# Moving weight sums and up items, and starting the sorted pairs five points sooner, in a routing attention and Strassen feed-forward kernel

## The chip, the core and the metric

The kernel runs on one core of one Trainium2 chip. The metric is the device time of one execution in microseconds (us). The engines of the core work in parallel, each on its own queue in order: TensorE (PE in the profile, its weight loads PEld), VectorE (DVE), ScalarE (ACT), GpSimd (POOL) and SyncE (SP), which here only issues DMAs. An instruction waits on semaphores for what it needs, and whatever stands behind it on its engine waits with it.

## What is computed

Attention with 4 batches, 8 heads, 768 tokens and 64 dimensions, in which a query sees only the keys of its own cluster (16 clusters per head, each token's cluster being the centroid with the largest product), and then a feed-forward layer with a hard swish:

```python
mask = q_assign[:, :, :, None] == k_assign[:, :, None, :]
scores = np.where(mask, 0.125 * q @ k.T, -1e9)      # per batch and head
attn = softmax(scores) @ v
x = attn.transpose(0, 2, 1, 3).reshape(3072, 512)
h = x @ w_in                                        # 512 -> 2048
g = h * np.clip(h + 3.0, 0.0, 6.0) / 6.0
out = g @ w_out                                     # 2048 -> 512
```

The weights come as 64-bit floats and are decoded on the chip.

## The kernel before

**Pairs.** Two heads make a pair: 16 pairs, four for each batch. Pairs 0 to 7 (batches 0 and 1) are done with full scores and a mask in a main loop; pairs 8 to 15 are sorted by cluster, so that a tile of 128 queries meets only three tiles of keys (a band).

**The main loop** (in `fast_path`) counts n in steps of two, 12 numbers for a pair. A step issues the scores, exponentials and key sums of two tiles (the key sums are adds on POOL, L430 and L433), the products with the values two tiles back, at two places per pair the division by the row sums (`sum_up`: products into a scratch bank, then reciprocal L473 and product L474 on VectorE), and the preparation of the next pair (`prep_items`: three turns of queries and keys into columns, L320, copied out by ScalarE, L326; cluster scores, L337; one hots, L348 to L357 and L379). The scratch of these, the `ph` of the up items and later X share the two banks of `psum_m`, in turn. Each step also issues a share of the weight decoding (five steps for each of 32 chunks: L232, L238, L248, L254 and L259 on VectorE, L228 and L244 on ScalarE), and at its end the eight half sums of w_out (`weight_sums`, L523).

**Feed-forward.** Tokens go through in 12 blocks of 256 (three per batch). A block is a list of 30 half items: 8 up items and 7 down items, each with a begin and an end. In the first block (u < 8) an up item is a plain product into `ph` (L597), a lift on ScalarE (L499) and a clip on VectorE (L502). In all others, up and down are done as 2 x 2 blocks with seven products instead of eight (Strassen and Winograd): an up item's begin makes `uX` and its end `uY` (L645), with sums on VectorE (L656), then lift, clip and the sums of g (`gated_sums`, L635). This needs the differences of w_in's blocks, `tx`, three tiles for each item. `make_first_sums` (L550 to L561) makes them once, after the first block's up items: three subtractions into `tx` and one in place in w_in (all L556), and a store to `td` in DRAM (L557). Later blocks load them from there (`first_sums`, L548). A down item multiplies g with blocks of w_out or with their differences T1 to T4 (L684); T3 replaces a block of w_out in place. X and Y are the two banks of sums. At the ends of parts 1, 3, 4 and 6 VectorE and ScalarE read them into y (L691, L735, L742), which SP stores (L695).

In the loop, the first block's up items are placed by counting (`want`): one each at n = 60, 64, 70, 74, 80, 84, 90, 94, always ahead of the preparation of that step; at n = 100 follows down item 0. The rest of the first block's down items come right after the loop. Their ends call `make_first_sums` (8 calls, in seven parts), before y is read.

**The late plan** (`steps_of`, `late_plan`). After the loop the order of the work is a list of points. Each point issues the operations of the sorted pairs that are due there and then one half item of the feed-forward (`fill`), except at "busy" points. A pair's operations have offsets from its slot; slot s starts at point AHEAD + 28 s, with AHEAD = 38, and in a slot the points 6 and 9 are busy, so that a slot has 26 half items. For a pair: its natural rows are loaded and turned (`load_natural`, `turn_natural`), cluster scores, one hots and running counts give each row's position (`order`, `positions`). `load_queries` and `load_keys` fetch the rows into one buffer each (L879, L885), `scatter` (L1014, 24 indirect DMAs on POOL) writes them to DRAM in sorted order, `load_ranked` (L870, L893) asks for them back and `turn_ranked` turns them. `band_scores` (L1057), `band_values` (L1096), `key_adds` (VectorE, L1110), `band_sums` (L1120) and `band_divide` (turns at L1133 and L1137, reciprocal and product xr at L1141 and L1144) make the result, `keep_ranked` stores it, `gather` (L1030, POOL) fetches it in natural order and `turn_back` turns it into columns of `xd`, from which blocks are loaded (L537). All turns go through `turn_piece` (L895 to L900): six transposes into a bank pair of `psum_s` and one copy on ScalarE. `psum_s` has one buffer in this stage, and band scores and `band_divide` use it too.

Pair 8 is the first (its early steps were done in the loop), pair 15 the last. After the last point the remaining half items follow.

Of the kernel before, what the change touches and what calls it, by code (L numbers as in the profile page):

```python
# [12 lines left out]
ALU = mybir.AluOpType  # L13
# [15 lines left out]
NFT = DFF // P  # L29
# [90 lines left out]
def fast_path(ctx, tc, ok, q, k, v, centroids, moe_w_in, moe_w_out, out):  # L120
# [3 lines left out]
    nc = tc.nc  # L124
# [53 lines left out]
    st = {}  # L178
# [329 lines left out]
    HF, HC = NFT // 2, DM // 2  # L508
# [38 lines left out]
            tx = st["tx", u] = txp.tile([P, 3, HK, P], F32, name="tx")  # L547
            nc.sync.dma_start(tx, td[:, i])  # L548

    def make_first_sums(i):  # L550

        tx = txp.tile([P, 3, HK, P], F32, name="tx")
        t1, t2, t4 = (tx[:, k] for k in range(3))
        b11, b12, b21, b22 = wi(0, 0, i), wi(0, 1, i), wi(1, 0, i), wi(1, 1, i)
        for out_, in0, in1 in ((t1, b12, b11), (t2, b22, t1), (t4, b21, t2), (b12, b22, b12)):
            nc.vector.tensor_tensor(out=out_, in0=in0, in1=in1, op=ALU.subtract)  # L556
        nc.sync.dma_start(td[:, i], tx)  # L557
        if i < 2:
            st["tx", HF + i] = tx

    def token_sums(b, m):  # L561

# [15 lines left out]
    def ffn_items(b):  # L578
        def up(m, i):
            u = (b * NHC + m) * HF + i  # L580
            g = g_sb[:, 0:4, i]
            got = {}

            def begin():
                raise_gates()
                load_block()
                if u >= HF:
                    first_sums(u + 2)
                    halved(b, m, u, i, got)

            def end():
                if u < HF:
                    ph = psum_m.tile([P, 512], F32, name="ph", tag="m")
                    for t in range(2):
                        f = t * HF + i
                        for kt in range(NKT):
                            nc.tensor.matmul(  # L597
                                ph[:, t * HC : (t + 1) * HC], lhsT=w_in_sb[:, kt, f * P : (f + 1) * P],
                                rhs=st["xb", b, m][:, kt], start=(kt == 0), stop=(kt == NKT - 1),
                            )  # L600
# [92 lines left out]
        def down(m, part):  # L693
            def keep(chunk, half, y, queue=nc.sync):
                queue.dma_start(out_v[b, 2 * m + chunk][:, half * HC : (half + 1) * HC], y)  # L695

            def multiply(second):
                if part < 2:
                    h = range(part * HF // 2, (part + 1) * HF // 2)
                    if second:  # L700
                        product(st["X"], 1, 5, st["T2"], False, True, False, h)
                    else:
                        product(st["X"], 0, 0, wb[0][0], True, False, False, h)
                    return
                kind, bank, half, w = (
                    (4, "Y", 0, st["T1"]), (1, "Y", 1, st["T3"]),
                    (2, "X", 0, wb[1][0]), (6, "Y", 0, wb[1][1]), (3, "Y", 1, st["T4"]),
                )[part - 2]
                h = range(second * HF // 2, (second + 1) * HF // 2)
                product(st[bank], half, kind, w, part == 2, part in (3, 4, 6), part > 3, h)  # L710

            def begin():
                raise_gates()
                if part == 0:
                    st["X"] = psum_m.tile([P, DM], F32, name="X", tag="m")
                    st["y0"] = yp.tile([P, DM], F32, name="y0", tag="y0")
                elif part == 2:
                    st["Y"] = st.get("psum_y", psum_m).tile([P, DM], F32, name="Y", tag="m")
                    st["y1"] = yp.tile([P, DM], F32, name="y1", tag="y1")
                multiply(0)  # L720

            def end():
                multiply(1)
                if part == 0:
                    finish()
                if (b, m, part) == (B - 1, NHC - 1, 6):
                    st["good"] = nc.values_load(ok[0:1, 0:1], min_val=0, max_val=1)
                if part == 4:
                    token_sums(*divmod(b * NHC + m + 1, NHC))
                if (b, m) == (0, 0):  # L730
                    for i in ([HF - 1, HF - 2], [5], [4], [], [3, 2], [0], [1])[part]:
                        make_first_sums(i)
                y0, y1 = st["y0"], st.get("y1")
                if part == 1:
                    nc.scalar.copy(out=y0[:, HC:], in_=st["X"][:, HC:])  # L735
                    add(y0[:, HC:], y0[:, HC:], st["X"][:, 0:HC])
                elif part == 3:
                    add(y1[:, 0:HC], y0[:, HC:], st["Y"][:, HC:])
                    add(y1[:, HC:], y1[:, 0:HC], st["Y"][:, 0:HC])
                    keep(1, 1, y1[:, HC:])  # L740
                elif part == 4:
                    nc.scalar.copy(out=y0[:, 0:HC], in_=st["X"][:, 0:HC])  # L742
                    keep(0, 0, y0[:, 0:HC])
                elif part == 6:
                    add(y1[:, 0:HC], y0[:, HC:], st["Y"][:, HC:])
                    keep(1, 0, y1[:, 0:HC])
                    add(y0[:, HC:], y0[:, HC:], st["Y"][:, 0:HC])

                    keep(0, 1, y0[:, HC:], nc.scalar if st["last"] else nc.sync)

            return [begin, end]

# [414 lines left out]
            load_block()  # L1167
            fill.extend(ffn_items(b))

    SLOT, AHEAD = 28, 38  # L1170

    def steps_of(g):

        first, last = g == FIRST, g == NPAIR - 1
        if first:
            plan = [
                (-38, load_queries), (-37, load_keys, 0), (-36, load_keys, 1), (-37, run_up),
                (-36, step_up), (-31, order), (-30, positions), (-20, lambda g: st.pop("signed")()),
            ]
        else:  # L1180
            plan = [
                (-46, load_natural, 0), (-45, load_natural, 1), (-38, turn_natural, 0), (-37, turn_natural, 1),
                (-36, cluster_scores), (-34, own_clusters), (-33, run_up), (-32, step_up), (-31, load_queries),
                (-29, order), (-28, positions), (-29, load_keys, 0), (-27, load_keys, 1),
            ]
        plan += [
            (-29 if first else -24, scatter, 0), (-29 if first else -24, scatter, 1), (-12, band_masks), (-3, load_ranked, 0), (-3, load_ranked, 1),
            (-2, load_ranked, 2), (-1, turn_ranked, 0), (0, turn_ranked, 1),
        ]
        d = 1 if last else 2  # L1190
        plan += [
            (d, band_scores, (0, 5), 1), (d + 2, band_scores, (2,), 3), (d + 4, band_scores, (4,)),
            (d + 4, band_values, 0), (d + 4, key_adds, 0, 1, 2), (d + 5, key_adds, 0, 3), (d + 7, band_values, 1),
            (d + 7, key_adds, 1, 1, 2), (d + 8, key_adds, 1, 3), (d + 10, band_sums),
            (12 if last else 14, band_divide), (14 if last else 16, keep_ranked),
            (15 if last else 23, gather), (28 if last else 37, turn_back),
        ]
        return [(g, *step) for step in plan]
# [29 lines left out]
    per_batch = NKT * per_pair  # L1228
    total = FIRST * per_pair
    lag_v, lag_d = 2, 4  # L1230
    up_first = NFT // 2
# [18 lines left out]
    st["early"] = st["free"] = True  # L1250
    st["last"] = st["moving"] = False
    fill, checks = [], []
    st["done"] = 0

    def check_all():
        now, checks[:] = checks[:], []
# [7 lines left out]
    with tc.manual_schedule():  # L1264
# [19 lines left out]
        for n in range(0, total + lag_d + 2, 2):  # L1284
# [16 lines left out]
            if r == 6:  # L1301
                load(g + 2, "q", "k")
                load(g + 1, "v")
            want = min(max(n + 2 - READY, 0) * up_first // (DECODED - READY) - st["done"], len(fill) // 2)
            st["done"] += want
            for i in range(max(len(prep), want)):
                if i < want:
                    fill.pop(0)()
                    fill.pop(0)()
                if i < len(prep):  # L1310
                    prep[i]()
            if n < total:
                for step in decode[: share(n, r)]:
                    step()
# [388 lines left out]
```

## Time and profile before

| | us |
|---|---|
| times of three runs | 956.59, 959.21, 961.89 |
| median | 959.21 |
| profiled execution | 959.56 |
| its span, first to last instruction | 957.8 |
| TensorE busy in the span | 929.6 |
| POOL busy | 576.3 |
| VectorE busy | 594.4 |
| ScalarE busy | 349.8 |

The granted TensorE clock was 0.998 throughout. A page shows one execution: what each engine did, who waited for whom, and what released a wait. A row of the timeline gives start, length, engine, line, operation, the tile written and the tiles read, the shapes and a count; in brackets stands the idle time of the engine just before and what ended it. A row of the waits gives the total, the number of times and the longest.

### The profile page before, as it was taken

Reading aid. Unit: us, or ns where it says so; the run is one execution under the profiler, and the core shown is the slowest. Engines: PE = TensorE matmul, PEld = TensorE weight load, DVE = VectorE, ACT = ScalarE, POOL = GpSimd, SP = SyncE. Lnnn points to the kernel's source line nnn. Section 1 sums busy time; section 2 is a strip of 40 time slices with the busy share of each in tenths; the row PEclk is TensorE's granted clock in tenths of the full one; section 3 lists DMA queues with packets and bytes.
Section 4 is the critical chain, followed back from the end, with each engine's and each line's share of the span. In section 5 each row is a group of like instructions: output and inputs, shape, how many; then the busy total and the mean of one; then the engine's idle time right before and its main releaser. Section 6 shows DMA issues by size and latency. Waiting matters only on the chain.

```text
span 957.8 us, 17621 instructions
## 1 busy us (share of the span) xinstructions
PE 929.6 (97%) x6358; PEld 725.5 (76%) x6358; DVE 594.4 (62%) x1306; ACT 349.8 (37%) x731; POOL 576.3 (60%) x1302
## 2 busy tenths in 40 slices
PE   8999999999899999999999999999999999999997
PEld 5444445555698798787897988888888799999996
DVE  6789888989977276274483474374471564636261
ACT  6888877765112232222232231241331311202020
POOL 3877767657367577776777878767777160303030
PEclk9999999999999999999999999999999999999999
DMA  7255464350474557456584484654744333323210
GB/s 206 90 133 155 132 176 124 106 145 10 145 223 137 151 159 164 129 130 153 153 198 119 120 204 118 160 155 114 198 142 95 102 96 116 102 72 105 66 57 26
DMA packets 174351, 124.23 MB, mean 130 GB/s; under 512 B 134064, under 2 KB 152496, under 8 KB 174256
## 3 DMA queue, kind: packets, MB, share of 16 engines
q1 hardware_dynamic: 164320, 109.86, 42.7%
q0 software_dynamic: 9216, 12.60, 4.4%
q8 instruction: 52, 0.85, 0.4%
q10 hardware_dynamic: 720, 0.56, 0.2%
q14 instruction: 43, 0.35, 0.1%
HBM read 94.67 MB, written 28.31 MB: 128 GB/s over the span
## 4 chain that ended last, share of the span: by engine, by line
PE 67%; DVE 3%; DMA 2%; issue 1%; ACT 0%; SPq 0%; another core or an unknown queue 0%; ACTq 0%; DVEq 0%
PE Y L684 17%; PE uY L645 15%; PE X L684 12%; PE uX L645 11%; PE pv L1096 3%; PE ps L899 3%; PE ps L1057 3%; DMA piece<-qd 2%; PE pv L1057 1%; PE pd L1120 1%; PE pcs L337 1%; PE rk L981 1%; PE ps L1137 1%; DVE tx L556 0%; DVE w_out_sb L523 0%
## 5 line engine op out<-in xcount | busy, mean ns | idle before, releaser
L433 POOL TENSOR_TENSOR acc<-acc,ex 128x768 f32<-128x768 f32 x64 | 123.3, 1927 | 37.4 <-ACT ex L423 33.9
L1014 POOL DMA_INDIRECT qd<-qn,pos x96 | 96.2, 1002 | 54.8 <-issue 17.5
L1030 POOL DMA_INDIRECT xn<-xsd,pos x96 | 94.3, 982 | 46.0 <-ACT sx L499 24.3
L499 ACT ACTIVATE sx<-g_sb,half_c 128x512 f32<-128x512 f32 x88 | 63.8, 725 | 146.5 <-DVE g_sb L656 126.3
L635 POOL TENSOR_TENSOR g_sb<-g_sb 128x256 f32<-128x256 f32 x52 | 41.8, 825 | 122.1 <-DVE g_sb L502 121.1
L1014 POOL DMA_INDIRECT kvd<-kvn,pos x96 | 96.1, 1001 | 27.3 <-issue 25.4
L1006 POOL MEMSET w_low<- 128x1 f32 x864 | 91.3, 106 | 33.3
L691 DVE TENSOR_TENSOR y<-y,Y 128x256 f32<-128x256 f32 x48 | 20.2, 421 | 132.7 <-PE Y L684 131.9
L684 PE MATMUL X<-w_out_sb,g_sb 128*128 128x256 f32 x384 | 90.4, 382 | 4.0 <-DVE y L691 2.2
L645 PE MATMUL uX<-xb,w_in_sb 128*128 128x128 f32 x704 | 93.0, 275 | 0.0
L684 PE MATMUL Y<-T,g_sb 128*128 128x256 f32 x384 | 88.0, 381 | 0.0
L684 PE MATMUL Y<-w_out_sb,g_sb 128*128 128x256 f32 x384 | 87.7, 380 | 0.0
L645 PEld LDWEIGHTS uX<-xb,w_in_sb 128*128 128x128 f32 x704 | 85.7, 192 | 0.0
L684 PEld LDWEIGHTS X<-w_out_sb,g_sb 128*128 128x128 f32 x384 | 70.9, 190 | 18.5 <-issue 4.0
L684 PEld LDWEIGHTS Y<-T,g_sb 128*128 128x128 f32 x384 | 72.1, 190 | 13.2 <-issue 3.9
L684 PEld LDWEIGHTS Y<-w_out_sb,g_sb 128*128 128x128 f32 x384 | 71.9, 190 | 10.6 <-issue 1.3
L656 DVE TENSOR_TENSOR sx<-uX,sx 128x128 f32<-128x128 f32 x176 | 51.1, 290 | 45.9 <-ACT sx L663 30.8
L400 PE MATMUL ps<-xf 64*128 64x384 f32 x384 | 78.5, 487 | 0.6 <-ACT ex L423 0.6
L423 ACT ACTIVATE ex<-ps 128x768 f32<-128x768 f32 x96 | 72.6, 802 | 4.5 <-PE ps L400 4.5
L443 PE MATMUL pv<-ex,vt 128*64 128x384 f32 x384 | 72.5, 499 | 0.0
L502 DVE SCALAR_TENSOR_TENSOR g_sb<-sx,g_sb 128x512 f32<-128x512 f32 x88 | 63.9, 728 | 3.3 <-ACT sx L499 2.3
L656 DVE TENSOR_TENSOR g_sb<-uY,sx 128x128 f32<-128x128 f32 (+1 forms) x176 | 65.6, 414 | 0.0
(194 smaller groups left out, 1796.7 us busy)
## 6 DMA issues: line engine op xcount, KB each, us to landing
tx<-td SPq DMA_DIRECT2D x86, 384.0 KB
raw<-in_moe_w_in_dram SPq DMA_DIRECT2D x16, 512.0 KB
raw<-in_moe_w_out_dram SPq DMA_DIRECT2D x16, 512.0 KB
xb<-xd SPq DMA_DIRECT2D x12, 512.0 KB
out_dram<-y SPq DMA_DIRECT2D x44, 128.0 KB
qk<-in_q_dram SPq DMA_DIRECT2D x18, 192.0 KB
qk<-in_k_dram SPq DMA_DIRECT2D x18, 192.0 KB
vt<-in_v_dram SPq DMA_DIRECT2D x16, 192.0 KB
```

Source lines behind the costliest of these rows:

```text
L400: nc.tensor.matmul(st["ps", n][:, t, 0:HALF], lhsT=x[r, NCH + j], rhs=x[r, hf * NHC : (hf + 1) * NHC], start=first, stop=last, skip_group_ ...
L423: nc.scalar.activation(out=ex, in_=sc, func=ACT.Exp, scale=SM_SCALE)
L433: nc.gpsimd.tensor_tensor(out=acc, in0=acc, in1=ex, op=ALU.add)
L443: nc.tensor.matmul(pv[t * D : (t + 1) * D], lhsT=vt[:, t, j], rhs=ex[:, t], start=(j == 0), stop=(j == NCH - 1),)
L499: nc.scalar.activation(out=r, in_=h, func=ACT.Relu, bias=half_c, scale=1.0 / 6.0)
L502: nc.vector.scalar_tensor_tensor(out=g, in0=r, scalar=1.0, in1=h, op0=ALU.min, op1=ALU.mult)
L645: nc.tensor.matmul(dst, lhsT=w[:, kt], rhs=x(kt), start=(kt == 0), stop=(kt == HK - 1))
L656: nc.vector.tensor_tensor(out=out_, in0=in0, in1=in1, op=ALU.add)
L684: nc.tensor.matmul(bank[:, half * HC : (half + 1) * HC], lhsT=g_sb[:, kind, i], rhs=w[:, i], start=(first and i == 0), stop=(last and i == ...
L1006: nc.gpsimd.memset(w_low, W_LOW)
L1014: i = nc.gpsimd.indirect_dma_start(out=rows[name, g, t], in_=src, in_offset=None, out_offset=bass.IndirectOffsetOnAxis(ap=pos[:, a, j, t : ...
L1030: nc.gpsimd.indirect_dma_start(out=xn[:, j, t], out_offset=None, in_=rows["xsd", g, t], in_offset=bass.IndirectOffsetOnAxis(ap=pos[:, 0, j ...
```

## The change

1. *Up items in the loop.* Their places are now a list, `up_at`; the fourth goes from n = 74 to n = 72. Where a step prepares with two turns (n = 60, 72, 84), the item stands between them instead of ahead.
2. *Sums of w_in.* `make_first_sums` is split: `kept_sums` makes the three subtractions and the store; the one in place stays where it was. The kept sums of items 7, 6, 5 and of 4 and 3 are made in the loop, ahead of the products of up items 0, 1, 2 and 5.
3. *Sums of w_out.* The halves of T1 and T2 stay at the end of the decoding; T3's go to the ends of down parts 0 and 1, T4's to those of parts 2 and 3.
4. *Reading y.* At the end of a down part, what reads X or Y is now issued ahead of these sums.
5. *Sorted pairs.* AHEAD is 33 instead of 38. Pair 8's early steps get offsets that keep their points, and its bands keep theirs (d = 7); its gather, turn back and masks come five points sooner, its band_sums and band_divide one.
6. *Rows.* Pairs 9 to 15 ask for sorted rows at offset -6 instead of -3, pair 8 two points sooner. Queries are asked for one point sooner within the slot, keys and values two, positions one.
7. *Last pair.* Its band_sums go from point 11 to 10 of its slot, and its turns of sorted rows one point sooner.
8. *Half items.* In slots 1, 2, 4, 5 and 6 point 6 is no longer busy: 27 half items. The late plan still issues 247 half items in all.

```diff
-    def make_first_sums(i):
+    def subtract(out_, in0, in1):
+        nc.vector.tensor_tensor(out=out_, in0=in0, in1=in1, op=ALU.subtract)
+
+    def kept_sums(i):

         tx = txp.tile([P, 3, HK, P], F32, name="tx")
         t1, t2, t4 = (tx[:, k] for k in range(3))
-        b11, b12, b21, b22 = wi(0, 0, i), wi(0, 1, i), wi(1, 0, i), wi(1, 1, i)
-        for out_, in0, in1 in ((t1, b12, b11), (t2, b22, t1), (t4, b21, t2), (b12, b22, b12)):
-            nc.vector.tensor_tensor(out=out_, in0=in0, in1=in1, op=ALU.subtract)
+        for sums in ((t1, wi(0, 1, i), wi(0, 0, i)), (t2, wi(1, 1, i), t1), (t4, wi(1, 0, i), t2)):
+            subtract(*sums)
         nc.sync.dma_start(td[:, i], tx)
         if i < 2:
             st["tx", HF + i] = tx
+        st["kept"].add(i)
+
+    def make_first_sums(i):
+        if i not in st["kept"]:
+            kept_sums(i)
+        subtract(wi(0, 1, i), wi(1, 1, i), wi(0, 1, i))
...
                 if u < HF:
+                    for other in sooner.get(u, ()):
+                        kept_sums(other)
                     ph = psum_m.tile([P, 512], F32, name="ph", tag="m")
...
-                if (b, m) == (0, 0):
-                    for i in ([HF - 1, HF - 2], [5], [4], [], [3, 2], [0], [1])[part]:
-                        make_first_sums(i)
                 y0, y1 = st["y0"], st.get("y1")
...
+                if (b, m) == (0, 0):
+                    for i in ([HF - 1, HF - 2], [5], [4], [], [3, 2], [0], [1])[part]:
+                        make_first_sums(i)
+                    if part in (0, 1):
+                        weight_sums(6 + part)
+                    elif part in (2, 3):
+                        weight_sums(2 + part)
...
-    SLOT, AHEAD = 28, 38
+    SLOT, AHEAD = 28, 33
...
-                (-38, load_queries), (-37, load_keys, 0), (-36, load_keys, 1), (-37, run_up),
-                (-36, step_up), (-31, order), (-30, positions), (-20, lambda g: st.pop("signed")()),
+                (-33, load_queries), (-32, load_keys, 0), (-31, load_keys, 1), (-32, run_up),
+                (-31, step_up), (-26, order), (-25, positions), (-15, lambda g: st.pop("signed")()),
...
-                (-36, cluster_scores), (-34, own_clusters), (-33, run_up), (-32, step_up), (-31, load_queries),
-                (-29, order), (-28, positions), (-29, load_keys, 0), (-27, load_keys, 1),
+                (-36, cluster_scores), (-34, own_clusters), (-33, run_up), (-32, step_up), (-32, load_queries),
+                (-31, load_keys, 0), (-29, order), (-29, positions), (-29, load_keys, 1),
             ]
+        d, e, f = (7, 18, 0) if first else (1, 12, -6) if last else (2, 14, -6)
         plan += [
-            (-29 if first else -24, scatter, 0), (-29 if first else -24, scatter, 1), (-12, band_masks), (-3, load_ranked, 0), (-3, load_ranked, 1),
-            (-2, load_ranked, 2), (-1, turn_ranked, 0), (0, turn_ranked, 1),
-        ]
-        d = 1 if last else 2
-        plan += [
+            (-24, scatter, 0), (-24, scatter, 1), (-12, band_masks), (f, load_ranked, 0), (f, load_ranked, 1),
+            (f + 1, load_ranked, 2), (d - 3, turn_ranked, 0), (d - 2, turn_ranked, 1),
             (d, band_scores, (0, 5), 1), (d + 2, band_scores, (2,), 3), (d + 4, band_scores, (4,)),
             (d + 4, band_values, 0), (d + 4, key_adds, 0, 1, 2), (d + 5, key_adds, 0, 3), (d + 7, band_values, 1),
-            (d + 7, key_adds, 1, 1, 2), (d + 8, key_adds, 1, 3), (d + 10, band_sums),
-            (12 if last else 14, band_divide), (14 if last else 16, keep_ranked),
+            (d + 7, key_adds, 1, 1, 2), (d + 8, key_adds, 1, 3), (e - 2, band_sums), (e, band_divide), (e + 2, keep_ranked),
             (15 if last else 23, gather), (28 if last else 37, turn_back),
         ]
...
-    decode += [lambda i=i: weight_sums(i) for i in range(8)]
+    decode += [lambda i=i: weight_sums(i) for i in range(4)]
+    st["kept"] = set()
+    sooner = {0: (7,), 1: (6,), 2: (5,), 5: (4, 3)}
+    up_at = (60, 64, 70, 72, 80, 84, 90, 94, 100)
...
-            want = min(max(n + 2 - READY, 0) * up_first // (DECODED - READY) - st["done"], len(fill) // 2)
-            st["done"] += want
-            for i in range(max(len(prep), want)):
-                if i < want:
-                    fill.pop(0)()
-                    fill.pop(0)()
-                if i < len(prep):
-                    prep[i]()
+            if len(prep) > 1:
+                prep.pop(0)()
+            if n in up_at:
+                fill.pop(0)()
+                fill.pop(0)()
+            for step in prep:
+                step()
...
-            busy = i >= AHEAD and (i - AHEAD) % SLOT in (6, 9)
+            slot, r = divmod(i - AHEAD, SLOT)
+            busy = slot >= 0 and (r == 9 or (r == 6 and slot not in (1, 2, 4, 5, 6)))
```

More of the change, by code (lines that the diff above doesn't have):

```diff
@@ L1230, in fast_path @@
     lag_v, lag_d = 2, 4
-    up_first = NFT // 2
     decode = [step for i in range(NW) for step in decoding_steps(i)]
-    decode += [lambda i=i: weight_sums(i) for i in range(8)]
+    decode += [lambda i=i: weight_sums(i) for i in range(4)]
+    st["kept"] = set()
+    sooner = {0: (7,), 1: (6,), 2: (5,), 5: (4, 3)}
+    up_at = (60, 64, 70, 72, 80, 84, 90, 94, 100)
     READY, DECODED = per_batch + 2 * lag_d, 2 * per_batch
@@ L1252, in fast_path @@
     fill, checks = [], []
-    st["done"] = 0
     def check_all():
```

## The prediction

> **What bounds the kernel now.** I read the page first, then the waits of TensorE, then the timelines of TensorE, VectorE and ScalarE around each wait.
>
> ```profile
> span 957.8 us, 17621 instructions
> PE 929.6 (97%) x6358; PEld 725.5 (76%) x6358; DVE 594.4 (62%) x1306; ACT 349.8 (37%) x731; POOL 576.3 (60%) x1302
> ```
>
> TensorE is busy for 929.6 of 957.8 us. The change gives it the same products, so all that can move is the other 28.2 us. The list of what TensorE waited for (total us, times, longest) says where most of that lies:
>
> ```profile
> PE ps L899 <- DMA piece<-qd: 4.5, 4, 2.1
> PE X L684 <- DVE y L691: 2.2, 1, 2.2
> PE X L684 <- DVE g_sb L502: 1.8, 1, 1.8
> PE pqk L320 <- ACT xf L326: 1.6, 2, 0.8
> PE ps L899 <- ACT xnat L900: 1.3, 1, 1.3
> ```
>
> The change bears on three of these five at once: rows asked for too late (4.5), X of the first block waiting until its old content is read (2.2), and two turns in the loop waiting for ScalarE's copy (1.6). With a wait of 0.75 shown below they sum to 9.0 us. The 1.8 for the last clip is a question of its own. All sums are made against the profiled execution, 959.56 us (1.76 us outside its span); the median shown is 959.21.
>
> **The loop: the moved items and sums.** The timeline of TensorE there (start, length, what ended the idle time before):
>
> ```profile
> 136.42 3.72 PE L597 MATMUL ph<-xb,w_in_sb 128*128 128x256 f32 x16
> 141.39 0.66 PE L320 MATMUL pqk<-ident,qk 128*128 128x128 f32 x4 [0.82 <-ACT xf L326]
> 173.39 1.09 PE L320 MATMUL pqk<-ident,qk 128*128 128x128 f32 x8
> 182.69 0.66 PE L320 MATMUL pqk<-ident,qk 128*128 128x128 f32 x4 [0.75 <-DVE rcp L473]
> 242.73 1.99 PE L684 MATMUL X<-w_out_sb,g_sb 128*128 128x256 f32 x8 [1.82 <-DVE g_sb L502]
> 259.02 1.99 PE L684 MATMUL X<-w_out_sb,g_sb 128*128 128x256 f32 x8 [2.21 <-DVE y L691]
> ```
>
> First part: the item now stands between two turns (n = 60, 72, 84). The second turn then shares its bank with the first turn, which was copied 3.6 us before, and no longer with ph: the 0.82 at 141.39 goes, and its twin at n = 84. Taking the fourth item out of n = 74 ends the 0.75 at 182.69. That is 2.4 us on TensorE. But VectorE runs in order, and in this stretch it is nearly full. ScalarE's lift and VectorE's clips, with the idle time before each:
>
> ```profile
> 140.18 0.69 ACT L499 ACTIVATE g_sb<-ph,half_c 128x512 f32<-128x512 f32 x1 [1.81 <-PE ph L597]
> 140.90 0.69 DVE L502 SCALAR_TENSOR_TENSOR g_sb<-g_sb,ph 128x512 f32<-128x512 f32 x1 [2.30 <-ACT g_sb L499]
> 154.80 0.69 DVE L502 SCALAR_TENSOR_TENSOR g_sb<-g_sb,ph 128x512 f32<-128x512 f32 x1 [2.15 <-ACT g_sb L499]
> 170.15 0.69 DVE L502 SCALAR_TENSOR_TENSOR g_sb<-g_sb,ph 128x512 f32<-128x512 f32 x1 [1.18 <-ACT g_sb L499]
> 173.65 0.69 DVE L238 SCALAR_TENSOR_TENSOR wtop<-raw,wtop 128x512 uint32<-128x512 uint32 x1
> 211.57 0.69 DVE L502 SCALAR_TENSOR_TENSOR g_sb<-g_sb,ph 128x512 f32<-128x512 f32 x1 [3.31 <-ACT g_sb L499]
> 228.63 0.69 DVE L502 SCALAR_TENSOR_TENSOR g_sb<-g_sb,ph 128x512 f32<-128x512 f32 x1 [0.51 <-ACT g_sb L499]
> 241.99 0.68 DVE L502 SCALAR_TENSOR_TENSOR g_sb<-g_sb,ph 128x512 f32<-128x512 f32 x1
> L556 DVE TENSOR_TENSOR tx<-w_in_sb,tx 128x256 f32<-128x256 f32 x16 | 6.9, 429 | 0.5
> ```
>
> A kept sum is three subtractions of 0.42 us, 1.25 us. Those of items 0, 1 and 2 go into idle times of 2.30, 2.15 and 1.18 us, and the pair at item 5 (2.5 us) into 3.31: hidden, and the cover just suffices (without it they cost 1.25 and 2.5). Their five stores to td now stand in SP's queue in the loop, each waiting for its subtractions; behind them stand loads of raw weights, asked for two chunks ahead of their use, which hides a wait of that length. What costs is the fourth item. At n = 72 its clip stands ahead of six decode steps, and it can't start before its product: 173.39 - 0.82 + 0.57 (one turn) + 3.76 (ph to lift, 136.42 to 140.18) + 0.72 (lift to clip) = 177.6. VectorE is done with the steps before it at 174.34 (173.65 + 0.69), so it idles about 3.3 us that it did not idle before; there the clip waited until after those steps. From 174.34 to the last clip at 241.99 it then had 67.65 us, of which 3.31 + 0.51 were idle and 63.8 work. After the change: 177.6 + 63.8 + 2.5 (the six subtractions before item 5's clip) = 243.9, if no idle time is left, since both idles are filled. The last clip is 2.0 us late, and X, which starts 0.74 us after it, goes from 242.73 to about 244.7. The 2.4 us that TensorE wins come back as waits for scratch banks that VectorE reads late (one hots, reciprocals) and for that clip. So I book **+2.0 us** here. The bounds come from VectorE's operations with two inputs in SBUF, which stretch when a POOL add is under way:
>
> ```profile
> 137.90 0.69 DVE L254 SCALAR_TENSOR_TENSOR wunit<-raw,wunit 128x512 f32<-128x512 uint32 x1
> 174.89 1.81 POOL L430 TENSOR_TENSOR acc<-ex 128x768 f32<-128x768 f32 x1 [4.53 <-ACT ex L423]
> 175.11 2.15 DVE L254 SCALAR_TENSOR_TENSOR wunit<-raw,wunit 128x512 f32<-128x512 uint32 x1
> ```
>
> Two of these stretched less often is 2.9 us less (-0.9); two more adds to wait for is 3.6 more (+5.6). The same operation takes 0.69 us by itself and 2.15 behind the add. [...]
>
> **The first block's down products.** Four of VectorE's eight half-sums of w_out and 15 of its 24 subtractions for tx leave the stretch after the last clip, and y's additions now stand ahead of what remains:
>
> ```profile
> 258.55 0.41 DVE L691 TENSOR_TENSOR y<-y,X 128x256 f32<-128x256 f32 x1
> ```
>
> X's second group waited until this addition, which stood behind 16.6 us of VectorE work after the last clip. In the new order only a reciprocal, a product, two subtractions, half of T3 and some small operations stand ahead, some 8 us; X's four rows like the 1.99 shown take over 7 us, so the addition runs as soon as X is done, and the bank is asked for only six groups of products later. T3 is needed at the seventh group and T4 at the thirteenth, 11 and 22 us after X's start at 1.8 us each; both are made earlier than that. The 2.2 us go: **-2.2**, with 0 as the other bound.
>
> **The sorted pairs: rows asked for sooner.** One ask, its scatter's last instruction and the turn that waits:
>
> ```profile
> 481.30 0.97 POOL L1014 DMA_INDIRECT kvd<-kvn,pos  x1 [0.16 <-issue]
> 489.74 1.01 SPq L870 DMA_DIRECT2D piece<-qd  x2
> 495.10 0.85 PE L899 MATMUL ps<-ident,piece 128*128 128x128 f32 x6 [0.85 <-DMA piece<-qd]
> ```
>
> The ask is 5.4 us ahead of its use and the transfer takes that; TensorE wanted it 0.85 us sooner. Three points more (about 5 us) cover the longest wait, 2.1. SP's queue is in order, and behind the ask stand tx loads; if the scatter weren't done, they would be held too. Here it ended at 482.3, 7.4 us before the ask. Pairs also start sooner (their slots have 5, 5, 4, 3, 3, 2, 1, 0 items less ahead of them), five slots are one item longer (1.3 to 1.8 us), and keys and values are asked for two points sooner, so POOL's chain of scatters and gathers moves at least as far as the asks. I book **-4.5**, bounds -5 and 0.
>
> The first pair is different. Its rows are asked for two points sooner too, but pair 9's six loads of queries, keys and values now stand ahead of them in SP's queue, and these wait for the first scatter to free their tiles:
>
> ```profile
> 297.53 10.76 SPq L870 DMA_DIRECT2D piece<-qd  x2
> 314.52 0.82 PE L899 MATMUL ps<-ident,piece 128*128 128x128 f32 x6
> ```
>
> SP already stands here until the scatter ends, about 308, and the rows are turned at 314.5 without a wait. Six asks of some 0.6 us put them at 311.6; with at least 4 us to landing (5.4 in the other pair) that is 315.6: **+1.0**, bounds 0 and 2.6.
>
> **What else the first and the last pair lose.** Last pair: band_sums moves from point 11 to 10 of its slot, ahead of an item that stood between it and key_adds:
>
> ```profile
> 759.36 0.61 PE L645 MATMUL uX<-xs,tx 128*128 128x128 f32 x4
> 760.79 0.83 PE L1120 MATMUL pd<-be,ones 128*32 128x384 f32 x2
> 762.44 0.85 PE L1120 MATMUL pd<-be,ones 128*32 128x384 f32 x6 [0.81 <-DVE be L1110]
> 761.96 0.42 DVE L1110 TENSOR_TENSOR be<-be 128x256 f32<-128x256 f32 x1
> ```
>
> VectorE's addition stays at 761.96; the item that TensorE did meanwhile (759.36 to 760.79) now comes after: **+1.4**. The first pair has the same order now (sums one point behind key_adds, formerly two): **+0.5**, between 0 and 1.4. And the first pair's band_divide now stands at the same point as the turn of pair 10's natural rows (both at point 51); they share the one buffer of psum_s, so TensorE must wait until VectorE has read it. Before, four items lay between. The same stretch now, with VectorE's queue at the same item:
>
> ```profile
> 343.75 0.85 PE L1120 MATMUL pd<-be,ones 128*32 128x384 f32 x8
> 346.92 0.61 DVE L656 TENSOR_TENSOR sx<-uX,sx 128x128 f32<-128x128 f32 x2
> 349.76 1.02 DVE L1144 TENSOR_TENSOR xr<-ps,inverses 128x384 f32<-128x384 f32 x2
> 407.82 0.38 PE L1137 MATMUL ps<-ident,bn 128*128 128x128 f32 x2
> 411.51 1.02 DVE L1144 TENSOR_TENSOR xr<-ps,inverses 128x384 f32<-128x384 f32 x2
> ```
>
> VectorE is through with item 2 at 347.5, 3.7 us after TensorE (343.75); with a reciprocal and xr (1.3) it frees the buffer after 5.0. TensorE fills 2.4 of these with uX and nine transposes: **+2.5**, bounds 1.0 (xr alone) and 4.3 (pair 9: 408.2 to 412.5).
>
> **Sum.** +2.0 - 2.2 - 4.5 + 1.0 + 1.4 + 0.5 + 2.5 = +0.7: 959.56 + 0.7 = **960.3 us**, 1.1 us above the median. Turns of natural rows in up items, where ScalarE's copy waited 1.3 once, are as many as before; I leave them at 0.
>
> **Rivals.**
> 1. VectorE keeps up at the fourth item. For it: in the loop's other items its idle time is 1.18 to 3.31 us, so it has slack somewhere. Against: at 182.69 TensorE already waits for its reciprocal. Then the loop's waits (0.82 + 0.75 + 0.82) and the 1.82 at X go: -4.2 in place of +2.0, in all -5.5: 954.1.
> 2. Slower: VectorE's lag in up items becomes the wait. TensorE's wait for rows let VectorE and ScalarE catch up; without it a turn meets ScalarE's copies that stand behind VectorE (the 1.3 for xnat). It decides where VectorE is over one item behind at a turn. Price: four pairs turn inside up items, 4 x 1.3, and 4.3 at point 51: 2.0 - 2.2 - 4.5 + 1.0 + 1.9 + 4.3 + 5.2 = +7.7: 967.3.
> 3. The asks don't do what they say: SP reaches them before the scatter is done, or transfers queue. The 4.5 stay: 964.8. Against it are the 7.4 us above.
>
> **Chances.** Forecast 0.5, rival 1 0.2, rival 2 0.2, rival 3 0.1. About 0.5% (4.8 us) is what a measurement here can tell from no change, so 954.4 to 964.0 counts as the same. Faster 0.2 (rival 1), same 0.5, slower 0.3 (rivals 2 and 3). The forecast's own range is 956 to 964.5; for 8 in 10 it must take in rival 3 and most of rivals 1 and 2, with some 1.5 us of spread: 952.5 to 968.
>
> **What would show it.** In the changed kernel X should start near 244.7 us, later than now, with idle time before it, and VectorE idle about 3 us at the fourth clip; waits of X for y and of turns for qd should be gone; new ones should stand at the turn of pair 10 (for VectorE's xr, about 2.5 us) and at the last pair's sums (over 2 us). I am wrong if X starts before 242, if waits for qd remain, or if turns wait for ScalarE in most pairs.

## The result, and the profile after

The changed kernel takes 965.0 us (median of 8 runs, 961.16 to 966.66) against 959.82 for the kernel before (8 runs, 956.59 to 961.89): a ratio of 1.0052, 95% interval 1.0035 to 1.0070. The forecast was 960.3, in a range of 952.5 to 968.0. So the kernel is slower by about 5 us where the forecast said 1, and inside its range. By the prediction's own measure (954.4 to 964.0 counts as the same) it is slower, an outcome to which it gave 0.3. The profiled execution has a span of 962.0 us, 4.2 more than before.

The head of the page, and the list of what TensorE waited for (total us, times, longest):

```profile
span 962.0 us, 17617 instructions
PE 932.9 (97%) x6358; PEld 728.8 (76%) x6358; DVE 593.3 (62%) x1306; ACT 349.9 (36%) x731; POOL 575.1 (60%) x1302
```

```profile
PE ps L913 <- issue: 2.7, 1, 2.7
PE X L694 <- DVE g_sb L502: 2.7, 2, 1.8
PE uX L655 <- DMA tx<-td: 2.3, 2, 1.8
PE ph L607 <- DVE one_hot L357: 2.3, 1, 2.3
PE pd L1134 <- DVE be L1124: 2.1, 1, 2.1
PE ps L913 <- ACT xnat L914: 1.9, 1, 1.9
```

Of the five waits that stood on the list of before, the one for y (2.2), those for qd (4.5) and those of the turns in the loop (1.6) are gone, as forecast. Others have come in their place, of nearly the same sum: TensorE's idle time is 29.1 us in place of 28.2. The other 3.2 us of the 4.2 stand in "busy": the same 6358 products took 932.9 us in place of 929.6. The timeline of TensorE at the new waits:

```profile
195.89 3.69 PE L607 MATMUL ph<-xb,w_in_sb 128*128 128x256 f32 x16 [2.34 <-DVE one_hot L357]
200.31 0.49 PE L379 MATMUL po<-ident_q,one_hot 128*128 128x128 bf16 x6 [0.72 <-DVE rcp L473]
...
243.19 1.13 PE L694 MATMUL X<-w_out_sb,g_sb 128*128 128x256 f32 x4 [1.82 <-DVE g_sb L502]
...
355.42 0.85 PE L913 MATMUL ps<-ident,piece 128*128 128x128 f32 x6 [2.75 <-issue]
...
557.41 0.68 PE L655 MATMUL uX<-xs,tx 128*128 128x128 f32 x4 [1.76 <-DMA tx<-td]
...
765.53 0.85 PE L1134 MATMUL pd<-be,ones 128*32 128x384 f32 x6 [2.15 <-DVE be L1124]
```

The row at 355.42 is the turn of pair 10 at point 51. "Issue" names no releaser; VectorE's timeline does, since its last read of the shared buffer ends at 355.3:

```profile
353.44 0.61 DVE L666 TENSOR_TENSOR sx<-uX,sx 128x128 f32<-128x128 f32 x2
353.97 0.22 DVE L1155 RECIPROCAL inverses<-pdt 128x12 f32<-128x12 f32 x1
354.29 1.02 DVE L1158 TENSOR_TENSOR xr<-ps,inverses 128x384 f32<-128x384 f32 x2
```

Where busy time grew shows in a table by stretch (us, TensorE busy and its products, granted clock, DMA share, GB/s), cut at the two moments at which the trace records a change of the granted clock (293.04 and 296.45), with as long a stretch on either side:

```profile
289.63:293.04 3.41, 1.49 (x14) 1.00 0.49 144
293.04:296.45 3.41, 3.41 (x20) 0.50 0.05 18
296.45:299.86 3.41, 3.41 (x32) 1.00 0.17 51
```

After a stretch in which TensorE was idle for 1.92 of 3.41 us (a turn at 292.60 waited for ScalarE's copy), the clock was 0.50 for the next 3.41 us: 20 products where 32 were done in the stretch after it. By that clock TensorE loses half of the stretch, 1.7 us. In the profile of before the clock stays at 1.00 until 954.15 us, after TensorE's last product (it ends at 951.26); the 0.998 given for it above is the mean over the execution.

### The profile page after: what moved, and what is told of

It is laid out like the page before. It is cut to its first block, busy times and chain, and to the rows that moved or that the text cites. A ratio compares the mean times of both kernels' runs of the same rounds, so it can differ in the third digit from the quotient of the medians.

```text
span 962.0 us, 17617 instructions
## 1 busy us (share of the span) xinstructions
PE 932.9 (97%) x6358; PEld 728.8 (76%) x6358; DVE 593.3 (62%) x1306; ACT 349.9 (36%) x731; POOL 575.1 (60%) x1302
## 4 chain that ended last, share of the span: by engine, by line
PE 67%; DVE 4%; DMA 1%; issue 1%; ACT 0%; SPq 0%; ACTq 0%
PE Y L694 17%; PE uY L655 15%; PE X L694 13%; PE uX L655 11%; PE pv L1110 3%; PE ps L1071 3%; PE ps L913 2%; PE pv L1071 1%; DMA tx<-td 1%; DVE g_sb L645 1%; PE pd L1134 1%; DVE g_sb L666 1%; DVE sx L666 1%; PE ps L1151 1%; DVE g_sb L502 1%
## 5 line engine op out<-in xcount | busy, mean ns | idle before, releaser
L433 POOL TENSOR_TENSOR acc<-acc,ex 128x768 f32<-128x768 f32 x64 | 123.8, 1935 | 34.3 <-ACT ex L423 30.7
L1044 POOL DMA_INDIRECT xn<-xsd,pos x96 | 96.4, 1004 | 63.1 <-DVE g_sb L645 31.6
L645 POOL TENSOR_TENSOR g_sb<-g_sb 128x256 f32<-128x256 f32 x52 | 38.1, 754 | 124.9 <-DVE g_sb L502 123.9
```

Of the source, the lines that this page charges most:

```text
L433: nc.gpsimd.tensor_tensor(out=acc, in0=acc, in1=ex, op=ALU.add)
L1044: nc.gpsimd.indirect_dma_start(out=xn[:, j, t], out_offset=None, in_=rows["xsd", g, t], in_offset=bass.IndirectOffsetOnAxis(ap=pos[:, 0, j ...
```

## The experiments

All ran on one chip, in three groups; the kernel before took 956.24, 956.03 and 956.41 us there (16 to 25 runs a group). The expectations of the first group were written against the 959.8 and 965.0 above, so what counts is the ratio to before, or the difference to the control (changed_again, 960.49), which is the changed kernel run once more. A ratio is the time over that of the kernel before in the same group, with its 95% interval in brackets. The diffs show the changed parts of the lines. Half of the change at a time came first.

**late_old.** The changed kernel with `SLOT, AHEAD`, `steps_of` and `busy` of before:

```diff
-    SLOT, AHEAD = 28, 33
+    SLOT, AHEAD = 28, 38
...
-            busy = slot >= 0 and (r == 9 or (r == 6 and slot not in (1, 2, 4, 5, 6)))
+            busy = i >= AHEAD and (i - AHEAD) % SLOT in (6, 9)
```

> The changed loop and sums, with the sorted pairs' points and busy points as before. Theory A (the loss is in the pairs' points: a shared buffer at point 51, the last pair's sums, loads of tx behind the rows, together over 5 us; the loop and sums win the 2.2 us that X waited for y and lose nothing): about 957.5 us, X starts near 243.2, X waits for y 0, waits for qd about 4.5 us. Theory B (the loop and the moved sums cost the time): about 964 us.

Measured: 953.65 us, ratio 0.9972 (0.9960 to 0.9984). X starts at 243.33. TensorE's list of waits has no y, and of qd and X it says:

```profile
PE ps L913 <- DMA piece<-qd: 4.9, 4, 2.1
...
PE X L694 <- DVE g_sb L502: 1.8, 1, 1.8
```

Theory A holds: the loop and the sums alone make the kernel faster, by 2.6 us.

**loop_old.** The kernel before with the changed `SLOT, AHEAD`, `steps_of` and `busy` (the diff above, the other way).

> The loop, the sums and the order of the first block as before, with the changed points of the pairs. Theory A: about 967 us (965.0 plus the 2.2 of X waiting for y), with waits for qd at 0 and the waits of about 2.7 us at point 51 and 2.1 us at the last pair's sums. Theory B: about 960 us.

Measured: 964.71 us, ratio 1.0087 (1.0074 to 1.0100), 8.5 us over before. X waits for y 2.2, pair 10's turn 2.75, the last pair's sums 2.15, and the first pair's rows 1.7 at 318 us. The loss lies in the pairs' points. The two halves (-2.6 and +8.5) sum to 5.9, the whole is 4.5 in the next group. The first pair's rows account for 1.3 of this 1.4: the turn waits 1.7 us for them here and 0.4 in the control.

**turn10_later.**

```diff
+        w = int(g == FIRST + 2)
...
-(-38, turn_natural, 0), (-37, turn_natural, 1), (-36, cluster_scores),
+(-38 + w, turn_natural, 0), (-37 + w, turn_natural, 1), (-36 + w, cluster_scores),
```

> The changed kernel with the turns of pair 10's natural rows and their cluster scores one point later (52, 53, 54), so that no turn stands at the point of the first pair's band_divide. Theory A (the turn waits 2.75 us for the buffer of psum_s that VectorE reads late): the wait goes or falls below 0.7 us, about 962.5 us. Theory B (VectorE lags here whatever the order, the wait comes back one item later): the wait for ACT or VectorE stays over 2 us near 355, about 965 us.

Measured: 958.32 us, ratio 1.0019 (1.0008 to 1.0030). The wait near 351 is 0.96 in place of 2.75. That is Theory A, though the wait doesn't fall below the 0.7 expected. The time is 2.2 us under the control below, for 1.8 of wait.

**sums_later.**

```diff
-(e - 2, band_sums)
+(e - 1 if last else e - 2, band_sums)
```

> The changed kernel with the last pair's band_sums one point later (11, as before), band_divide still at 12. Theory A: the wait for be falls from 2.15 us to about 0.8, about 963.7 us. Theory B (the late wait moves to the divide, one item behind): the sum of waits between 760 and 775 us stays above 1.8 us, about 965 us.

Measured: 957.87 us, ratio 1.0018 (1.0007 to 1.0029). The wait for be is 0.82 in place of 2.15, and nothing comes behind it: 2.6 us under the control for 1.3 of wait. Both edits gave somewhat more than their wait, but by less than the control's time is known to (its interval is some 1.8 us to either side). That made me look at the mean granted clock, which each run records: 0.9975 over the 25 runs of before, 0.9959 in turn10_later and 0.9969 here.

**changed_again**, no edit.

> The changed kernel as it is, as a control beside the others of this group, with the granted clock of every run. Both theories: ratio about 1.005 to before. [...]

Measured: 960.49 us, ratio 1.0048 (1.0029 to 1.0066), mean clock 0.9957 against 0.9976 for the 16 runs of before in this group. In those 16 runs the clock sorts the times: the 11 runs at 0.998 or 0.999 lie between 954.3 and 957.0, the five at 0.995 or 0.996 between 957.4 and 957.9. The table by stretch of this profile, and TensorE's timeline there (at the half rate 4 products take 1.06 us, elsewhere 0.61):

```profile
347.75:351.17 3.42, 0.86 (x8) 1.00 0.07 22
351.17:354.58 3.41, 3.41 (x18) 0.50 0.00 1
354.58:357.99 3.41, 3.41 (x32) 1.00 0.97 229
```

```profile
350.31 0.84 PE L913 MATMUL ps<-ident,piece 128*128 128x128 f32 x6 [2.75 <-issue]
...
351.68 1.06 PE L655 MATMUL uY<-xb,w_in_sb 128*128 128x128 f32 x4
```

So a lower clock went with a longer time. One stretch of 3.41 us at half rate lowers the mean clock by 0.0018 (half of 3.41 over the span of 957.4). At 1.7 us for such a stretch, that would be about 0.95 us for each 0.001 of clock; in the times a step of clock goes with about 0.65 us for each 0.001, so by the times the stretch is worth about 1.2 us rather than 1.7. The control's mean clock lies 0.0019 below that of before: about one such stretch more in an execution. Theory C of the runs below is that with a wait the stretch at half rate behind it goes too.

**both_fixes**, the edits of turn10_later and sums_later together.

> The changed kernel with pair 10's turns one point later and the last pair's sums one point later. If only the waits count (2.75 to about 1.0, 2.15 to 0.8): 3.1 us under the control, ratio about 1.002. Theory C (with the waits their half-rate windows go too): 4.5 to 6.5 us under the control, ratio 0.998 to 1.000, and a mean clock of 0.997 or more.

Measured: 956.48 us, ratio 0.9999 (0.9989 to 1.0009), clock 0.9972. It is 4.0 us under the control, of which the two waits are 3.1. Both forecast steps are confirmed, and the two points alone are the difference between slower and the same. The 4.0 lies between the two expectations, and the 0.9 beyond the waits is within the noise, so whether any of it is clock isn't settled by this run.

**rows_late**, the asks of all pairs but the first at the old point.

```diff
-        d, e, f = (7, 18, 0) if first else (1, 12, -6) if last else (2, 14, -6)
+        d, e, f = (7, 18, 0) if first else (1, 12, -3) if last else (2, 14, -3)
```

> The changed kernel with the ranked rows asked for at the old point (three points before the pair's slot; the first pair's ask is not touched). Forecast's step: the waits for qd come back with about 4.5 us, less the wait for tx of 1.7 that stands behind the earlier asks: 2.8 us over the control or more, ratio about 1.008. Rival (the earlier start of the pairs' chain alone moves the rows, or the loads of tx lose as much as the asks gain): within 1 us of the control.

Measured: 970.8 us, ratio 1.0158 (1.0143 to 1.0172), 10.3 over the control, far beyond both. From the list of TensorE's waits:

```profile
PE ps L913 <- DMA piece<-qd: 9.7, 7, 4.7
```

SP's timeline ahead of the longest of these waits:

```profile
598.49 13.34 SPq L705 DMA_DIRECT2D out_dram<-y  x4
612.01 0.84 SPq L893 DMA_DIRECT2D qn<-in_q_dram  x2
612.89 0.43 SPq L548 DMA_DIRECT2D tx<-td  x1
613.42 0.97 SPq L884 DMA_DIRECT2D piece<-qd  x2
614.50 3.59 SPq L884 DMA_DIRECT2D piece<-kvd  x2
```

Pair 13's rows are asked for at 613.4, though their scatter's last instruction ended at 598.9. The first row is four stores of y, issued at 598.5, 602.8 and, the last two, from 611.0: SP stood there until y was made. The next pair's queries are ahead too; the turn then waited until 619.69. With these points the sooner ask is needed, and for another reason than I gave: to get ahead of the stores. (Waits for qd are 9.3 us above the control's 0.4.)

**rows_loads_late**, that edit and the next pair's loads at their old points:

```diff
-(-32, load_queries), (-31, load_keys, 0), (-29, order), (-29, positions), (-29, load_keys, 1),
+(-31, load_queries), (-29, order), (-28, positions), (-29, load_keys, 0), (-27, load_keys, 1),
```

> The changed kernel with the rows asked for at the old point and the next pair's queries and keys too. Theory (in the run with only the rows late the next pair's loads stood ahead of the rows in SP's queue, which made the waits for qd 9.3 us instead of 4.5): the waits for qd fall to 4 to 5 us, about 964 us. Rival (the waits come from the five half items more in the slots and from the earlier start): they stay above 8 us, about 970 us.

Measured: 963.67 us, ratio 1.0076 (1.0057 to 1.0096); waits for qd 6.0 (9.7 above). Most of the theory holds: the loads moved ahead of the rows make 3.7 of the 9.7. The remaining 6.0 is over the 4 to 5 expected.

**late_old_rows**, late_old with `f = -3 if first else -6` for the asks.

> The changed loop and sums, the pairs at their old points, and only the ranked rows of all pairs but the first asked for three points sooner. Forecast's step alone: the waits for qd (4.9 us in the profile of the kernel with the old points) go to 0, about 949 us, and with them some half-rate windows. Rival (the six asks then stand ahead of loads of tx, and products wait for those instead, as at 553 us of the changed kernel, 1.5 us): about 951 us or more.

Measured: 953.65 us, ratio 0.9966 (0.9954 to 0.9978), the same median as late_old. The waits for qd are gone. The first line of TensorE's list of waits, and SP's timeline ahead of the longer of the two:

```profile
PE uX L655 <- DMA tx<-td: 3.8, 2, 3.1
```

```profile
602.39 1.05 SPq L884 DMA_DIRECT2D piece<-qd  x2
603.54 1.13 SPq L884 DMA_DIRECT2D piece<-kvd  x2
604.72 0.83 SPq L548 DMA_DIRECT2D tx<-td  x1
605.59 1.24 SPq L907 DMA_DIRECT2D vs<-kvd  x2
606.92 0.78 SPq L548 DMA_DIRECT2D tx<-td  x1
607.88 1.48 SPq L893 DMA_DIRECT2D qn<-in_q_dram  x2
609.46 0.74 SPq L548 DMA_DIRECT2D tx<-td  x1
```

The rival is right: the rows, values and queries stand in one queue with the up items' tx. Asked for sooner, they make tx late, and the products wait for tx (3.1 us at 610.66) instead of the turn for qd (2.1 at 611.54 in late_old). Waits of 4.9 became waits of 3.8. The other 1.1 may have gone to the clock, whose mean is 0.9966 here and 0.9980 in late_old; no run settles that.

**late_fourth**, late_old with `up_at = (60, 64, 70, 74, ...` in place of 72.

> The changed loop with the fourth item at n = 74 as before, the pairs at their old points. Forecast's step (the fourth clip at n = 72 costs VectorE idle time and X 2.0 us): X starts 1 to 2 us sooner than 243.3 and the time is 952 us. Rival (what VectorE idles there it has as slack, since the last clip waits for work that comes later): X within 0.5 us of 243.3, and the 0.75 us wait for a reciprocal at the turn behind the item is back; 953.5 to 954.5 us.

Measured: 952.33 us, ratio 0.9956 (0.9941 to 0.9970). X starts at 241.85, 1.5 sooner, of which 0.3 arose in the first 9 us. TensorE's timeline, in place of the waits of 2.34 and 0.72 above:

```profile
182.90 0.66 PE L320 MATMUL pqk<-ident,qk 128*128 128x128 f32 x4 [1.30 <-DVE rcp L473]
...
198.96 0.49 PE L379 MATMUL po<-ident_q,one_hot 128*128 128x128 bf16 x6 [0.36 <-DVE rcp L473]
```

So the fourth item costs about 1.3 us at n = 72: the traces show it, while the intervals of the two ratios still touch. This version has the lowest median of the study, 4 us under the kernel before.

**late_kept_out**, late_old with `sooner = {}`: all sums in the first block.

> The pairs at their old points, the items and the order of y as changed, but no kept sums in the loop: all of them are made in the first block's down products. Forecast's step (VectorE has no idle time left ahead of the last clip, and the six subtractions at item 5 with their collision cost 4.0 us): X starts 2 to 4 us sooner than 243.3; if nothing is given back, 951.5 us. Rival (the sums made later hold up y's additions or the loads of tx in the up products): X sooner, but waits for y or tx of over 1 us between 250 and 300, 953 us or more.

Measured: 956.18 us, ratio 0.9993 (0.9981 to 1.0004). X starts at 243.35, as in late_old: the subtractions in the loop cost X nothing. In the first block Y waits 0.5 for a half sum and uX 0.9 for tx, and waits for qd are 5.4. Neither expectation holds for X; by the times the sums are 2.5 us better in the loop. About 1 us of these 2.5 shows as waits. The mean clock of the profiled run is 0.997 here and 0.998 in late_old; how much of the rest is clock stays open.

**keep_busy**: TensorE is given something to do in two waits.

```diff
+                if g == NPAIR - 1 and (t, hf) == (0, 0):
+                    spare = st["psum_y"].tile([P, P], F32, name="spare", tag="m")
+                    for _ in range(10):
+                        nc.tensor.transpose(out=spare, in_=ident, identity=ident)
...
+        if g == FIRST:
+            spare = st["psum_y"].tile([P, P], F32, name="spare", tag="m")
+            for _ in range(12):
+                nc.tensor.transpose(out=spare, in_=ident, identity=ident)
```

> The changed kernel with 12 transposes into a spare tile of the up products' second pool of banks, ahead of pair 10's turn at point 51, and 10 more between the first pair of sums and the rest in the last pair's band_sums; their results go nowhere. Theory C: they lie inside the waits of 2.75 and 2.15 us, so that the turn and the sums start where they did, TensorE's idle time there falls to about 1 us, half-rate windows become fewer, the clock rises by 0.001 to 0.002 and the time falls by 1 to 2 us against the control. Rival (half-rate windows have nothing to do with waits, or cost nothing): the same clock, and the time of the control or up to 2 us over it.

Measured: 960.92 us, ratio 1.0045 (1.0031 to 1.0058), clock 0.9962 (control: 960.49 and 0.9957). The time doesn't fall, so as a gain this failed. The table by stretch says why, in two pairs of stretches:

```profile
347.98:351.39 3.41, 1.97 (x19) 1.00 0.07 23
351.39:354.81 3.42, 3.42 (x33) 1.00 0.43 104
549.42:552.84 3.42, 0.99 (x10) 1.00 1.10 310
552.84:556.25 3.41, 3.41 (x19) 0.50 1.18 272
```

At point 51 TensorE is now idle 1.44 us of the stretch, and the clock stays at 1.00 behind it, while in the control it fell. But TensorE was idle for 2.43 us of the stretch from 549.42 in this execution (its longest wait for tx is 2.4), and the half rate came behind it. So one half-rate stretch was kept away and another came; that fewer of them make the kernel faster rests on the clocks and times above, and no edit has shown it.

## Why the prediction was right or wrong

| step | forecast | measured |
|---|---|---|
| loop, up to the start of X | +2.0 | +0.5, of which 0.4 arose in the first 9 us |
| X waiting for y | -2.2 | -2.2 |
| turns waiting for qd | -4.5 | -4.5 |
| what stands behind the sooner asks | 0 | +1.9 (waits for tx 2.3, formerly 0.4 at that place for VectorE) |
| first pair's rows | +1.0 | 0 in the profile, 0.4 in the control |
| last pair's sums | +1.4 | +1.3 |
| first pair's sums | +0.5 | +0.9 (busy time of pd, 8.5 in place of 7.6) |
| pair 10's turn at point 51 | +2.5 | +2.75 |
| natural rows' copies by ScalarE | 0 | about 0 (1.9 here, formerly 2.1) |
| a second block's last clip | 0 | +0.8 |
| half rate of TensorE's clock | 0 | +1.7 in the profile |
| sum | +0.7 | +3.1 of 4.2 |

The remaining 1.1 are small differences in busy time and gaps that no row names.

Two of these rows, the copies and the half rate, belong to this execution rather than to the change. Here is one stretch of TensorE in this profile, and the same stretch in the control's, which is of the same kernel:

```profile
280.00:293.00 13.00, 10.38 (x81) 1.00 0.53 153
280.00:293.00 13.00, 12.96 (x116) 1.00 0.51 153
```

Followed product by product, the two profiles differ by at most 0.2 us up to 280, and at 296 the control is 5.4 us ahead. This profile has slow products (four of uY take 0.90 us at 280.54 and 0.92 at 284.39, elsewhere 0.61) and short gaps from 280.5 to 287 (some 2 us), then the wait for ScalarE's copy (1.92), then the half rate; the control has none of them there, and its half rate comes at point 51. The profile of before has such a place as well: from 408 to 435 it loses 3.7 us against late_old, whose pairs have the same points, and its waits for the copies stand there. In none of the other 12 profiles does TensorE wait for them. Rival 2 took its 1.3 for each turn from that place. What makes such a place stays open; 3.7 us is about what lies between the 959.82 of before in the result and its 956.0 to 956.4 in the later groups, but which executions have one isn't known. The two losses happen to be nearly equal, so the row for the copies reads 0; and the +1.7 stands for the changed kernel only in so far as the control has one such stretch too.

**The places were right.** The shared buffer, the last pair's sums and y came out to within 0.3 us, and undoing the first two of these took away what they cost.

**The loop was mis-sized.** VectorE did idle at the fourth clip, but 1.90 us in place of 3.3, since the sum kept ahead of the third clip had made it later. Then I added 66.3 us of work and reached 243.9. The clips in VectorE's timeline of the changed kernel:

```profile
178.09 0.69 DVE L502 SCALAR_TENSOR_TENSOR g_sb<-g_sb,ph 128x512 f32<-128x512 f32 x1 [1.90 <-ACT g_sb L499]
...
213.73 0.68 DVE L502 SCALAR_TENSOR_TENSOR g_sb<-g_sb,ph 128x512 f32<-128x512 f32 x1
229.10 0.69 DVE L502 SCALAR_TENSOR_TENSOR g_sb<-g_sb,ph 128x512 f32<-128x512 f32 x1 [0.19 <-ACT g_sb L499]
242.47 0.67 DVE L502 SCALAR_TENSOR_TENSOR g_sb<-g_sb,ph 128x512 f32<-128x512 f32 x1
```

From 178.09 to 242.47 are 64.4 us, and at 229.10 VectorE still waits for ScalarE: the premise that no idle time is left failed by a little. That clip belongs to the item at n = 90. From it to the last one are 13.4 us of VectorE work in a row, in the changed kernel as before (228.63 to 241.99), and X follows at once. So X starts 14 us after that clip, which goes by TensorE's item at n = 90: VectorE's lag earlier in the loop counts only where TensorE waits for it. That is why late_kept_out moved nothing. In the sum, the clip at n = 72 was right (177.6 forecast; 178.09 measured, with the 0.4 of the first 9 us in it), and the 66.3 was the term that was too large. The subtractions at item 5 did meet a POOL add (two of them took 2.38 us from 210.18, while the add ran for 1.98 us from 210.30; the next two, with no add under way, took 0.89), but the decoding was stretched less: its nine L254 between the clip at n = 72 and the last took 10.0 us in place of 12.9. In the profile of before, L254 took 0.87 to 2.30 us in the 19 cases in which it began 0.3 us or more ahead of the end of a running add (L430 or L433), and 0.68 to 0.75 in the other 13. L259, which has two inputs in SBUF too, took 0.68 to 0.69 in all 32, of which 18 began under an add: the prediction's words on such operations fit L254 and not L259. What the fourth item costs is what TensorE waits: 2.34 and 0.72 in place of 1.30 and 0.36, 1.4 us; the waits of the two turns that went are 1.6, so the two nearly cancel.

**The asks were right in the wait and wrong in the gain.** "Transfers queue" stood in rival 3, with a chance of 0.1. I priced the sooner asks by the turn that waits and not by the tx loads that stand behind them, though the forecast named those loads. With the old points that takes the whole gain in time (late_old_rows). Rival 3's price, 964.8, lies beside the measured 965.0 by luck: it had the 4.5 of waits for qd stay, and they went.

**Not foreseen** were the half rate, and the wait of 0.8 at 308 us (also in the control, 0.9): pair 9's run counts, 2.1 us of VectorE, now stand ahead of a block's last clip. VectorE's timeline of the changed kernel:

```profile
305.51 0.87 DVE L946 TENSOR_TENSOR runs<-runs,oh 128x64 bf16<-128x64 bf16 x4
...
306.64 0.65 DVE L946 TENSOR_TENSOR steps<-steps 128x64 bf16<-128x64 bf16 x3
307.32 0.23 DVE L946 TENSOR_TENSOR upto<-steps 128x128 bf16<-128x128 bf16 x1
307.46 0.69 DVE L502 SCALAR_TENSOR_TENSOR g_sb<-sx,g_sb 128x512 f32<-128x512 f32 x1
```

So the forecast's 1 us came from errors that partly cancel: the loop 1.5 and the first pair's rows 1.0 too dear, tx, clip and clock 4.4 too cheap, all three put at nothing in the sum. That the time lies inside the range is in part luck.

## What to carry to other kernels

Price an earlier load by what stands behind it in its queue, not only by the wait that it ends: a queue in order turned one wait into another here (in late_old_rows, waits of 4.9 us for rows into 3.8 for tx). Before work is moved to another point, list which buffers the operations of that point share; two points that were off by one made this change slower instead of the same. And a wait can cost more than itself: behind that of 2.75 us in the control the clock was 0.50 for 3.41 us, which is 1.7 us of TensorE's work.

## What the runs showed of the hardware

The tables by stretch show the granted clock at 0.50 for 3.41 us three times while TensorE had work: from 293.04 in the changed kernel and from 351.17 in the control, with 1.00 behind it, and from 552.84 in keep_busy. In the 3.41 us ahead of these TensorE was idle for 1.92, 2.56 and 2.43 us. A stretch of the same length with 1.98 us idle had no fall behind it, in the table of sums_later:

```profile
348.06:351.48 3.42, 1.44 (x13) 1.00 0.06 19
351.48:354.89 3.41, 3.41 (x33) 1.00 0.41 112
```

So idle time in such a stretch alone doesn't sort the four. Nor does the length of the wait: one of 2.75 us had a fall behind it in the control, where it ends at 350.31, and none in the changed kernel, where it ends at 355.42. What decides isn't shown.

Runs of one kernel spread without any edit: the 16 of before in the control's group lie between 954.34 us (mean clock 0.999) and 957.86 (0.996). A stretch of 3.41 us at 0.50 is 1.7 us of TensorE's work by that clock, and about 1.2 us of the time by these 16 runs.
